# Strassen's quarter products for six of the sixteen feature tiles of a feed-forward layer's first part

## The chip, the core and the metric

The kernel runs on one core of a Trainium2 chip. A core has a matrix engine (PE, with its weight loads shown apart as PEld), three engines for element-wise work (DVE, ACT, POOL) and queues that issue transfers (here nearly all on SP). Every engine works through its instructions in the order in which the program issued them; what one engine needs of another it waits for. PE writes to PSUM, from where ACT or DVE copies results to SBUF. The metric is the time of one execution on the device in microseconds (us); lower is better.

## The reference

The input is q, k and v (8 batches, 8 heads, 576 positions, 64 features, float32) and a threshold `tau`. Attention with a threshold comes first, then a feed-forward layer on its output:

```python
scores = scale * np.matmul(q, k.transpose(0, 1, 3, 2))
thresh = np.max(scores, axis=-1, keepdims=True) - tau
scores = np.where(scores >= thresh, scores, -1000000000.0)
attn = np.exp(scores - np.max(scores, axis=-1, keepdims=True))
attn = attn / (np.sum(attn, axis=-1, keepdims=True) + 1e-09)
x = np.matmul(attn, v)                 # heads side by side: (8, 576, 512)

xn = (x - mean(x)) / np.sqrt(var(x) + 1e-06) * g_ln
out = x + np.maximum(xn @ w_ch1, 0.0) @ w_ch2      # 512 -> 2048 -> 512
```

## The kernel before, in words

**Slots and stages.** Attention is cut into 72 slots, nine to a batch (s = 0 to 8). In a slot, PE multiplies q and k for one piece of the batch's heads (scores, L390, 2.2 us); DVE takes the row maxima (L404) straight from PSUM; ACT takes exponentials (L415) with these as bias; DVE masks by the threshold and sums (L422); POOL scales by the reciprocal sums (L438); DVE transposes 32 x 32 blocks (`turn_blocks`, L498 and L504) into `et`; SP writes `et` to a scratch in memory and reads it back in another order in the next slot (`fetch`: `em`, and the last 64 positions into `rests`); in the last stage of that next slot PE multiplies with v (`values_of`, L550). Four slots of a batch also hold `turn` (L338 to L351), which prepares the next q and k. The first batch turns its weights with PE instead. Each slot is issued in four stages, 0 to 3: stage 0 ends between the second and the third exponential, stage 1 comes before the masks, stage 2 before the slot's transposes, stage 3 after them.

**Groups.** The feed-forward layer runs on 16 groups of 288 positions, two to a batch (even and odd), with features on the partitions. Its steps fill PE between the attention's products. `centre` subtracts the mean (`xc`, L599). `first_part` makes `hidden`, 16 tiles of 128 features: for each tile d, four products (one for each 128 input features, `product`, L101) into one PSUM bank, and an eviction by ACT with ReLU (L729). On the side it makes the variance: squares by ACT (L735), three sums by POOL (L737), a product with a constant (`var`), and an inverse square root by DVE in three rounds (`root`, L661 to L669).

The second part (`second_quarters`, all groups but the first) already uses Strassen's scheme: the 2 x 2 blocks of `w_ch2` (rows, columns) and of `hidden` (feature halves, early and late 144 positions) are combined so that seven block products, not eight, are needed. Sums of the weights are made once (`differences`, L706). Sums of `hidden` are made in place for each group: `t3` and `t4` on POOL, `t2` and `t1` on DVE (L797). Each of the seven products is a segment of 16 products of 144 columns. Then sums of their results (`u`, `22`, `21`, `11`, `12`, L816), scaling by the inverse root and adding x (`finish`: `done11`, `hi`, `done12` on POOL, L824 and L816), and output transposes on DVE (`store`: `o2`, `o3`, `o0`, `o1`, L643), after which SP sends them out (L650).

**The order.** PSUM has two banks for tiles, segments and the mean and variance products together (`ps_ff`, two buffers). A step to PE can therefore be started only when the step before the last has been evicted. The number of units issued in each stage follows a written rule (`second_part`, L900): what is left of the group, times the stage's share (0.6, 1.0, 1.25, 0.35), over the shares left until the next group is ready. A product of 288 columns is one unit, one of 144 columns half a unit; a group has 121 units.

Element-wise calls of a group wait in one queue, `drops`, in the order in which they were queued. `drip` (L608) takes them out at the end of stage 1 (only as far as an urgent call stands in the queue, and then with all that stand ahead of it), at the end of stage 2 (for up to 4 calls on DVE and 6 cost units on POOL) and of stage 3 (2 on DVE); before the masks only urgent calls for POOL go out. `need` takes out calls until a named one has gone. The order of a slot, shortened:

```python
diags = weights(es, thr, blocks_go)      # masks (DVE), scaling (POOL)
run_all(aside)
drip()                                   # end of stage 1
...
second_part(n, 2)
...
scr = turn_blocks(s, es)                 # the slot's transposes (DVE)
...
run_all(aside)                           # rounds of the root
drip({nc.vector: 4, nc.gpsimd: 6})       # end of stage 2
```

Of the kernel before, what the change touches and what calls it, by code (L numbers as in the profile page):

```python
# [18 lines left out]
def kernel(  # L19
# [39 lines left out]
    J = 4  # L59
# [7 lines left out]
    BIG = 3.0e38  # L67

# [19 lines left out]
    rests = [consts.tile([128, 4, 128], F32, name=f"rest{i}") for i in range(2)]  # L88
# [61 lines left out]
    for t in rests + v_rest:  # L150
        nc.gpsimd.memset(t, 0.0)
# [244 lines left out]
    def exponentials(n):  # L396
# [5 lines left out]
        for h in range(2):  # L402
            i = slice(2 * h, 2 * h + 2)
            nc.vector.tensor_reduce(  # L404
                out=neg[:, i], in_=pairs[h],
                axis=AXL.X, op=ALU.max, negate=True,
            )
            nc.gpsimd.tensor_scalar(  # L408
                out=thr[:, i], in0=neg[:, i], scalar1=-1.0, scalar2=low_sb,
                op0=ALU.mult, op1=ALU.add,  # L410
            )
        for i in range(4):
            if i == 2:
                yield es, thr
            nc.scalar.activation(es[:, i], blocks[i], func=AF.Exp, bias=neg[:, i : i + 1])  # L415

    def weights(es, thr, divide):
# [13 lines left out]
        for i in range(4):  # L431
            if not divide:
                if i % 2 == 0:
                    two = ffn.tile([128, TOK], F32, tag="o", bufs=4, name="diag")
# [14 lines left out]
    def turned_tiles(s):  # L449
        return att.tile([128, 4, J, 128], F32, tag="em", bufs=1, name="em"), rests[s % 2]  # L450
# [81 lines left out]
    def values_of(b, s, turned_weights):  # L532
# [23 lines left out]
        if s == HP:  # L556
            for t in range(2):
# [4 lines left out]
                for c in range(1, NK):  # L562
                    add_feature(2 * b + t, c, slice(QH, TOK))
        else:
# [3 lines left out]
            if hp:  # L568
                add_feature(g, hp, slice(0, QH))

    def add_feature(g, c, cols):

        x = groups[g]
        if g not in sums:
            sums[g] = ffn.tile([128, TOK], F32, tag="sum", bufs=2, name="sum")
# [59 lines left out]
    def add_to_x(g, m, p2, rb):  # L635
        o = ffn.tile([128, TOK], F32, tag="o", bufs=4, name="o")
# [4 lines left out]
    def store(eng, g, m, o):  # L641
        ot = ffn.tile([128, TOK], F32, tag="o", bufs=4, name="ot")
# [35 lines left out]
    HT, HD, HM = TOK // 2, ND // 2, NK // 2  # L678
# [5 lines left out]
    }  # L684
    more = []

    def differences():
# [5 lines left out]
        for t in (flat[:, :size], flat[:, size : 2 * size], flat4[:, :size]):  # L693
            more.append(t.rearrange("p (m d c) -> p m d c", m=HM, d=HD))
        s2, s3, s4 = more
# [13 lines left out]
    def first_part(g):  # L709
# [3 lines left out]
        rb = sq = None  # L713
        plain = g == 0
        sums_of = differences() if g == 1 else iter(())
        for d in range(ND):
            while conversion.ended < 4 * (d // 4 + 1):
                yield 0, 0
            while d == ND - 2 and len(rooted) <= g:
                run_all(aside)  # L720
# [9 lines left out]
            next(sums_of, None)  # L730
            yield 2, 1
            if sq is None and d and (plain or part > 1 or d == ND // 2 - 1):
                squared = d
                sq = hidden[:, ND - NK :]
                nc.scalar.activation(sq, xc, func=AF.Square)  # L735
                for c in range(1, NK):
                    nc.gpsimd.tensor_tensor(out=sq[:, 0], in0=sq[:, 0], in1=sq[:, c], op=ALU.add)  # L737
            elif sq is not None and rb is None and (
                d >= squared + (7 if plain else 3) and part > (0 if plain else 1)
                or d == ND - NK - 1  # L740
            ):
                var = ps_ff.tile([128, TOK], F32, tag="ff", name="var")
                product(var, lhsT=avg_sb, rhs=sq[:, 0], start=True, stop=True)
                rb = ffn.tile([128, TOK], F32, tag="rb", bufs=2, name="rb")
                nc.scalar.activation(sq[:, 2], var, func=AF.Identity, bias=eps_sb)
                aside.append(lambda: root(rb, sq[:, 2], sq[:, 3]))
                yield 1, 1
        for _ in sums_of:
            pass
        return rb  # L750

    def second_plain(g, rb):
        for m in range(NK):
# [10 lines left out]
            aside.append(lambda m=m, p2=p2: add_to_x(g, m, p2, rb))  # L764
            yield 2, 1

    def second_quarters(g, rb):
# [7 lines left out]
        drip(everything=True)  # L775
# [3 lines left out]
        done = set()  # L779

        def later(*calls, urgent=None):
            for what, cost, fn, eng, *args in calls:

                def go(what=what, fn=fn, eng=eng, args=args):
                    fn(eng, *args)
                    done.add(what)

                drops.append((urgent, now, eng, cost, go))

        def need(*what):  # L790
            while not done.issuperset(what):
                drops.pop(0)[-1]()

# [5 lines left out]
        def segment(weights, rhs, out=None):  # L799
# [10 lines left out]
            if out is None:  # L810
                out = ffn.tile([128, HM, HT], F32, tag="part", bufs=4, name="part")
            nc.scalar.copy(out, bank)  # L812
            return out

        def add(eng, out, a, b):
            eng.tensor_tensor(out=out, in0=a, in1=b, op=ALU.add)  # L816
# [11 lines left out]
        later(("t3", 3, by_fours, pool, b12, b22, b12, ALU.subtract), urgent=pool)  # L828
        banks_taken[0] = True
        yield from segment(w2[0, 0], b11, y11)  # L830
        need("t3")
        later(("t2", 3, by_fours, dve, b11, b11, b12, ALU.add), urgent=dve)
        yield 2, 0.5
        p2 = yield from segment(w2[0, 1], b21)
        need("t2")
        later(("t4", 3, by_fours, pool, b21, b21, b11, ALU.subtract), urgent=pool)
# [3 lines left out]
        yield from segment(s2, b11, y21)  # L840
        need("t4")
        later(("t1", 3, by_fours, dve, b11, b22, b11, ALU.subtract), urgent=dve)
# [218 lines left out]
```

## Time and profile before

| | |
|---|---|
| median of 3 runs | 1398.09 us (1396.95 to 1398.28) |
| profiled execution | 1397.5 us, span 1395.7 us |
| busy: PE, DVE, POOL, ACT | 1337.3, 931.2, 609.7, 460.4 us |
| products of 288 columns, tiles of the first part (`p<-xc,w`, 4 records each) | 4096 records, 518.1 us |
| products of 144 columns, segments (`seg<-hidden`, 4 records each) | 6720 records, 436.4 us |
| evictions with ReLU on ACT (L729) | 256, 414 ns each |
| copies of segments on ACT (L812) | 105, 400 ns each |
| sums of 288 columns, POOL (L816) and DVE (L668) | some 800 ns and 499 ns each |
| mean granted clock of PE | 0.993 |

The span is the time from the first to the last instruction; the profiled execution's own time is 1.8 us longer. One product shows as four records (two halves of the output columns, two records each), whose busy times overlap. In a line of the timeline the columns are start, duration, engine, line, operation, output and inputs, shape and count; in brackets stands how long the engine was idle just before and what ended it. After the first batch the kernel repeats: the row maxima of slots nine apart start 160.6 us apart.

### The profile page before, as it was taken

Reading aid. Unit: us, or ns where it says so; the run is one execution under the profiler, and the core shown is the slowest. Engines: PE = TensorE matmul, PEld = TensorE weight load, DVE = VectorE, ACT = ScalarE, POOL = GpSimd, SP = SyncE. Lnnn points to the kernel's source line nnn. Section 1 sums busy time; section 2 is a strip of 40 time slices with the busy share of each in tenths; the row PEclk is TensorE's granted clock in tenths of the full one; section 3 lists DMA queues with packets and bytes.
Section 4 is the critical chain, followed back from the end, with each engine's and each line's share of the span. In section 5 each row is a group of like instructions: output and inputs, shape, how many; then the busy total and the mean of one; then the engine's idle time right before and its main releaser. Section 6 shows DMA issues by size and latency. Waiting matters only on the chain.

```text
span 1395.7 us, 35606 instructions
## 1 busy us (share of the span) xinstructions
PE 1337.3 (96%) x15048; PEld 986.9 (71%) x15048; DVE 931.2 (67%) x1638; ACT 460.4 (33%) x923; POOL 609.7 (44%) x809
## 2 busy tenths in 40 slices
PE   4888999999999999999999999999999999999996
PEld 3665665867768596877869586776858677685966
DVE  5998967676776767657776767657775767766211
ACT  3877613232332323232232323323232323323120
POOL 2444444544433454343444455353444444334413
PEclk8999999999999999999999999999999999999998
DMA  9722355447744476446754477445764476443211
GB/s 231 175 77 70 95 145 153 154 146 187 196 133 159 136 191 180 142 137 185 192 160 146 150 196 188 138 148 151 187 180 143 134 183 184 127 161 129 63 18 18
DMA packets 316383, 205.48 MB, mean 147 GB/s; under 512 B 242368, under 2 KB 273856, under 8 KB 308160
## 3 DMA queue, kind: packets, MB, share of 16 engines
q1 hardware_dynamic: 311456, 202.62, 50.8%
q8 instruction: 118, 1.93, 0.6%
q10 hardware_dynamic: 4736, 0.59, 0.4%
q14 instruction: 41, 0.34, 0.1%
q0 software_dynamic: 32, 0.00, 0.0%
HBM read 119.41 MB, written 83.76 MB: 146 GB/s over the span
## 4 chain that ended last, share of the span: by engine, by line
PE 89%; DVE 5%; ACT 2%; issue 1%; POOL 0%; POOLq 0%; DVEq 0%; ACTq 0%
PE p L101 36%; PE seg L101 30%; PE sc L550 10%; PE sc L390 10%; DVE e L422 1%; PE tp L101 1%; DVE neg L404 1%; PE var L101 0%; PE mean L101 0%; DVE w L269 0%; ACT e L415 0%; PE tr L478 0%; ACT part L812 0%; DVE hidden L296 0%; DVE w L296 0%
## 5 line engine op out<-in xcount | busy, mean ns | idle before, releaser
L101 PE MATMUL p<-xc,w 128*64 128x288 f32 x4096 | 518.1, 408 | 13.0 <-ACT hidden L729 5.5
L101 PEld LDWEIGHTS p<-xc,w 128*64 128x64 f32 x4096 | 288.9, 137 | 224.6 <-ACT hidden L729 16.0
L404 DVE TENSOR_REDUCE neg<-sc 128x2 f32<-128x1152 f32 x144 | 188.8, 1352 | 271.1 <-PE sc L390 271.0
L415 ACT ACTIVATE e<-sc,neg 128x576 f32<-128x576 f32 x288 | 196.8, 744 | 247.7 <-DVE neg L404 247.7
L438 POOL TENSOR_SCALAR e<-e,den 128x576 f32<-128x576 f32 x252 | 194.1, 783 | 134.5 <-DVE den L427 134.3
L101 PE MATMUL seg<-hidden,w 128*64 128x144 f32 x3840 | 248.0, 287 | 0.0
L101 PEld LDWEIGHTS seg<-hidden,w 128*64 128x64 f32 x3840 | 235.1, 137 | 11.6 <-issue 7.7
L422 DVE SCALAR_TENSOR_TENSOR e<-sc,thr,e 128x576 f32<-128x576 f32 x288 | 222.0, 810 | 13.9 <-ACT e L415 13.2
L729 ACT ACTIVATE hidden<-p 128x288 f32<-128x288 f32 x256 | 105.9, 414 | 241.0 <-PE p L101 239.2
L408 POOL TENSOR_SCALAR thr<-neg,low_sb 128x2 f32<-128x2 f32 x144 | 42.5, 295 | 306.1 <-DVE neg L404 302.1
L390 PE MATMUL sc<-kT,qT 64*128 64x384 f32 (+3 forms) x1024 | 150.6, 425 | 20.1 <-DVE qT L350 10.1
L504 DVE STREAM_TRANSPOSE et<-e 128x1152 f32<-128x1152 f32 x112 | 153.1, 1374 | 14.8 <-POOL e L438 14.0
L390 PEld LDWEIGHTS sc<-kT,qT 64*128 64x128 f32 x1024 | 94.3, 191 | 69.9 <-issue 18.2
L550 PE MATMUL sc<-em,v_in 128*64 128x256 f32 (+1 forms) x1408 | 130.8, 329 | 0.0
L101 PE MATMUL seg<-hidden,stage 128*64 128x144 f32 x1920 | 123.1, 286 | 0.0
L101 PEld LDWEIGHTS seg<-hidden,stage 128*64 128x64 f32 x1920 | 117.9, 137 | 3.5 <-issue 2.3
L550 PEld LDWEIGHTS sc<-em,v_in 128*64 128x64 f32 x1408 | 86.4, 137 | 32.2
L797 POOL TENSOR_TENSOR hidden<-hidden 128x576 f32<-128x576 f32 x60 | 84.4, 1426 | 27.3 <-ACT hidden L729 19.0
L576 POOL TENSOR_TENSOR sum<-sum,x 128x256 f32<-128x256 f32 (+1 forms) x64 | 32.6, 509 | 113.2 <-ACT x L567 110.7
L797 DVE TENSOR_TENSOR hidden<-hidden 128x576 f32<-128x576 f32 x60 | 49.1, 853 | 47.8 <-PE seg L101 38.1
L567 ACT COPY x<-sc 128x256 f32<-128x256 f32 x60 | 22.3, 372 | 164.7 <-PE sc L550 115.3
L812 ACT COPY part<-seg 128x288 f32<-128x288 f32 x75 | 30.1, 401 | 131.2 <-PE seg L101 109.6
(151 smaller groups left out, 1186.6 us busy)
## 6 DMA issues: line engine op xcount, KB each, us to landing
scr<-et SPq DMA_DIRECT2D x63, 1152.0 KB, 4.9
em<-scr SPq DMA_DIRECT2D x63, 1024.0 KB, 5.9
out_dram<-ot SPq DMA_DIRECT2D x256, 36.0 KB, 4.9
q_in<-in_q_dram SPq DMA_DIRECT2D x124, 72.0 KB, 2.7
k_in<-in_k_dram SPq DMA_DIRECT2D x120, 72.0 KB, 3.0
rest<-scr SPq DMA_DIRECT2D x63, 128.0 KB, 6.0
v_in<-in_v_dram SPq DMA_DIRECT2D x28, 256.0 KB, 5.2
w<-in_moe_w_ch_dram SPq DMA_DIRECT2D x10, 512.0 KB, 6.2
```

The lines of the kernel that those rows point to most:

```text
L101: nc.tensor.matmul(out[r], lhsT=lhsT[:, r], rhs=rhs, **flags)
L390: nc.tensor.matmul(sc[h][64 * i : 64 * i + 64 if s == HP else 128, at : at + n], lhsT=ql[r] if s == HP else qT[r, half, j * 128 : (j + 1) ...
L404: nc.vector.tensor_reduce(out=neg[:, i], in_=pairs[h], axis=AXL.X, op=ALU.max, negate=True,)
L408: nc.gpsimd.tensor_scalar(out=thr[:, i], in0=neg[:, i], scalar1=-1.0, scalar2=low_sb, op0=ALU.mult, op1=ALU.add,)
L415: nc.scalar.activation(es[:, i], blocks[i], func=AF.Exp, bias=neg[:, i : i + 1])
L422: nc.vector.scalar_tensor_tensor(out=es[:, i], in0=blocks[i], scalar=thr[:, i : i + 1], in1=es[:, i], op0=ALU.is_ge, op1=ALU.mult, accum_o ...
L438: nc.gpsimd.tensor_scalar(out=es[:, i], in0=es[:, i], scalar1=den[:, i : i + 1], scalar2=1.0, op0=ALU.mult, op1=ALU.mult,)
L504: nc.vector.transpose(et[:, :, 64 * h : 64 * h + 64].rearrange("p n (j c) -> p j n c", j=2), es[:, 2 * h : 2 * h + 2].rearrange("p j (n c) ...
L550: nc.tensor.matmul(dst[64 * h : 64 * h + 64], lhsT=vt[:, h, c, :] if c < J else vr[:, h, :], rhs=pick(em[:, :, c] if c < J else er, hp, h) ...
L576: nc.gpsimd.tensor_tensor(out=sums[g][:, cols], in0=x[:, 0, cols] if c == 1 else sums[g][:, cols], in1=x[:, c, cols], op=ALU.add,)
L729: nc.scalar.activation(hidden[:, d], p1, func=AF.Relu)
L797: eng.tensor_tensor(out=out[at], in0=in0[at], in1=in1[at], op=op)
```

## The change

Tiles 5, 6, 7 and 13, 14, 15 of the first part are made by Strassen's scheme, like the second part. The 2 x 2 blocks are of `w_ch1` (256 input features by 384 features) and of `xc` (256 input features by 144 positions). Seven quarter products `Q1` to `Q7` of six products of 144 columns each take the place of 24 products of 288 columns. Group 0 keeps whole tiles.

- Weight sums are made once, in group 1, into tiles of their own (`w1_more`); one of them is in place. `differences` is stepped three times a tile instead of once.
- Sums of `xc` go into parts of `hidden` not yet in use: `xt3`, `xt2`, `xt4` (POOL, queued as urgent when the quarters start) and `xt1` (DVE).
- Results are copied by ACT without ReLU and combined by `xu2`, `xu3`, `x21`, `x12`, `xu4`, `x22` (DVE) and `x11` (POOL); `r11` (POOL), `r21`, `r12`, `r22` (DVE) clamp them at zero.
- The ten whole tiles run first; from the third on, one quarter product follows each.
- A group has 118 units.
- The variance may start one stage earlier (`part` instead of `part > 1`), and its product one tile earlier.
- The second part no longer empties the queue at its start; some of its results go straight into `y`.
- To make room: one tile for the remainders instead of two (`er`), one `sum` buffer instead of two, two `part` buffers of 432 columns instead of four of 288, and no `o` buffers: the output transposes write into the group's x tile. Sums for the last 32 positions of an odd group move from s = 4 to s = 6. From the second batch on there is a second place in each slot where finished outputs are sent.

```diff
-    rests = [consts.tile([128, 4, 128], F32, name=f"rest{i}") for i in range(2)]
+    er_sb = consts.tile([128, 4, 128], F32, name="er")
...
+        if s == HP + 2:
+            add_rest(g)
...
-            sums[g] = ffn.tile([128, TOK], F32, tag="sum", bufs=2, name="sum")
+            sums[g] = ffn.tile([128, TOK], F32, tag="sum", bufs=1, name="sum")
...
-        ot = ffn.tile([128, TOK], F32, tag="o", bufs=4, name="ot")
+        ot = groups[g][:, m]
...
+            for k in range(NK // 2):
+                s1 = of(1, 0, k)
+                nc.gpsimd.tensor_tensor(out=s3[k], in0=of(0, 0, k), in1=s1, op=ALU.subtract)
+                yield
+                nc.vector.tensor_tensor(out=s1, in0=s1, in1=of(1, 1, k), op=ALU.add)
+                nc.vector.tensor_tensor(out=s2[k], in0=s1, in1=of(0, 0, k), op=ALU.subtract)
+                nc.gpsimd.tensor_tensor(out=s4[k], in0=of(0, 1, k), in1=s2[k], op=ALU.subtract)
+                yield
...
+        def norm(must=False):
+
+            if ended and not squared and (plain or part):
+                squared.append(ended)
+                nc.scalar.activation(sq, xc, func=AF.Square)
+                for c in range(1, NK):
+                    nc.gpsimd.tensor_tensor(out=sq[:, 0], in0=sq[:, 0], in1=sq[:, c], op=ALU.add)
+            elif squared and not rb and (
+                ended >= squared[0] + (7 if plain else 2) and part > (0 if plain else 1) or must
+            ):
+                var = ps_ff.tile([128, TOK], F32, tag="ff", name="var")
+                product(var, lhsT=avg_sb, rhs=sq[:, 0], start=True, stop=True)
...
+        def quarter(q, weights, rhs, out=None):
+            bank = ps_ff.tile([128, size, HT], F32, tag="ff", name="quarter")
+            for k in range(half):
+                for m in range(size):
+                    at, end = (k, m), (half - 1, size - 1)
+                    product(
+                        bank[:, m], lhsT=weights[k][:, m * 128 : (m + 1) * 128], rhs=rhs[:, k],
+                        start=at == (0, 0), stop=at == end,
+                    )
+                    if at != end:
+                        yield 1, 0.5
+            if out is None:
+                out = part_tile("part")[:, : size * HT].rearrange("p (m t) -> p m t", t=HT)
+                parts[q] = out
+            nc.scalar.copy(out, bank)
+            yield 2, 0.5
+
+        def quarters():
+            later(
+                done, ("xt3", 1, less, pool, t3, b22, b12), ("xt2", 1, add, pool, t2, b11, t3),
+                ("xt4", 1, less, pool, t4, b21, t2), urgent=pool,
+            )
+            yield quarter(1, old(0, 0), b11, h11)
+            yield quarter(2, old(0, 1), b21)
+            need(done, "xt4")
+            yield quarter(7, s3, t3)
+            later(done, ("xt1", 1, less, dve, t1, b12, b11), urgent=dve)
+            yield quarter(6, s2, t2, h12)
+            later(
+                done, ("xu2", 1, add, dve, h12, h12, h11), ("xu3", 1, add, dve, parts[7], parts[7], h12),
+                ("x11", 1, add, pool, h11, h11, parts[2]), ("r11", 1, positive, pool, h11),
+            )
+            need(done, "xt1")
+            yield quarter(4, old(1, 1), t4, h21)
+            later(done, ("x21", 1, add, dve, h21, h21, parts[7]), ("r21", 1, positive, dve, h21))
+            need(done, "x11")
+            yield quarter(3, s4, b22)
+            later(done, ("x12", 1, add, dve, h12, h12, parts[3]))
+            yield quarter(5, old(1, 0), t1, h22)
+            later(
+                done, ("xu4", 1, add, dve, h12, h12, h22), ("r12", 1, positive, dve, h12),
+                ("x22", 1, add, dve, h22, h22, parts[7]), ("r22", 1, positive, dve, h22),
+                urgent=dve,
+            )
...
+        for d in singles:
...
+            yield from tile_of(d)
+            for _ in range(1 if plain else 3):
+                next(sums_of, None)
+            ended += 1
+            yield from norm()
+            if not plain and d > 1:
+                yield from next(between, ())
+                yield from norm()
...
-        drip(everything=True)
...
-    STEPS = [1 + NK * ND * 2] + [1 + NK * ND * 2 - NK * ND // 8] * (NG - 1)
+    STEPS = [1 + NK * ND * 2] + [
+        1 + NK * ND * 2 - NK * ND // 8 - sum(NK * len(ms) for ms in SETS) // 4
+    ] * (NG - 1)
...
+        if n >= SLOTS:
+            run_first(stores)
```

## The prediction

> **What bounds the kernel now.** I read the head of the page, then the time by stretches, the chain that ended last, and the timeline of single slots. The head:
>
> ```profile
> span 1395.7 us, 35606 instructions
> PE 1337.3 (96%) x15048; PEld 986.9 (71%) x15048; DVE 931.2 (67%) x1638; ACT 460.4 (33%) x923; POOL 609.7 (44%) x809
> ```
>
> PE is busy 96% of the span. One batch of nine slots, as a stretch (columns: stretch, length, busy time and instructions of PE, PEld, DVE, ACT, POOL, clock, DMA):
>
> ```profile
> 530.60:691.20 160.60, 159.97 (x1826) 118.49 (x1824) 109.37 (x196) 47.51 (x96) 72.47 (x100) 1.00 0.56 163
> ```
>
> So a batch is as long as PE's work in it. DVE has 51 us to spare, but on average only. The chain in order of time shows PE alone, with these prices:
>
> ```profile
> 1171.79 11.79 PE p L101 x96
> ...
> 1355.84 27.46 PE seg L101 x448
> ```
>
> 96 matmul records are 24 products of 288 columns: 11.79 / 24 = 0.491 us. 448 are 112 products of 144 columns: 27.46 / 112 = 0.245 us.
>
> DVE in a slot of s = 2, where an odd group begins (its scores ended at 368.75):
>
> ```profile
> 368.92 2.62 DVE L404 TENSOR_REDUCE neg<-sc 128x2 f32<-128x1152 f32 x2 [2.93 <-PE sc L390]
> ...
> 376.83 1.38 DVE L504 STREAM_TRANSPOSE et<-e 128x1152 f32<-128x1152 f32 x1
> 378.49 1.38 DVE L504 STREAM_TRANSPOSE et<-e 128x1152 f32<-128x1152 f32 x1 [0.28 <-POOL e L438]
> 379.79 1.96 DVE L816 TENSOR_TENSOR y<-y,part 128x288 f32<-128x288 f32 x3
> 384.53 0.84 DVE L643 STREAM_TRANSPOSE ot<-y 128x288 f32<-128x288 f32 x2 [2.78 <-POOL y L816]
> 386.16 0.48 DVE L643 STREAM_TRANSPOSE ot<-y 128x288 f32<-128x288 f32 x1 [0.79 <-POOL y L816]
> 386.95 2.62 DVE L404 TENSOR_REDUCE neg<-sc 128x2 f32<-128x1152 f32 x2 [0.31 <-PE sc L390]
> ```
>
> Here DVE has 0.31 us left before the next row maxima, though it stood still 2.78 and 0.79 us in front of the output transposes, which wait for POOL. ACT in the next slot:
>
> ```profile
> 388.41 1.37 ACT L415 ACTIVATE e<-sc,neg 128x576 f32<-128x576 f32 x2 [3.24 <-DVE neg L404]
> 389.67 0.41 ACT L729 ACTIVATE hidden<-p 128x288 f32<-128x288 f32 x1
> ```
>
> The eviction that frees PE's PSUM bank stands behind two exponentials, and these behind the maxima. There are two banks, so maxima that come late stop PE.
>
> **The gain.** Fifteen groups each lose 24 products (24 x 0.491 = 11.8 us) and get 42 half-width ones (42 x 0.245 to 0.248 = 10.3 to 10.4): 1.4 us each, 21 us in all, all of it on PE's path.
>
> **What else is added.** ACT: six evictions of 0.41 become seven of 432 columns, 0.50 by interpolation between 288 (0.40) and 512 (0.59): 1.0 us a group on an engine busy 47.5 of 160.6. DVE a group: one sum of 288 (0.45), six of 432 (0.58, between 0.45 and 0.70), three clampings (0.4 by L661's 0.37): 5.1 us. POOL: three of 288 (0.80), one of 432 (1.1), one clamping (0.6): 4.1 us. By throughput this fits; its place decides.
>
> **Without cost.** One remainder tile instead of two: its fetch stands on SP behind that of `em`, which has one tile and waits for the same slot's reads. One `sum` tile: the mean's product has read it before the next group's first sum. The output transposes write the group's own x tile, which the third group after needs: the last send goes in the slot s = 4 (odd) or s = 8 (even), the tile is written again at the earliest in stage 3 of the slot after an even group's or two slots after an odd one's; SP has the same 256 sends, two send points a slot. `part` with two buffers: each is read out a segment before it is due. The exponentials keep their order.
>
> **Where it lands: odd groups.** The pacing rule (L900) issues a group's units by fixed shares. In the slot s = 2 it gives 8, 5, 11, 4 units in stages 0 to 3; the trace's 24 products in a row there are 8 + 5 + 11. With 118 units instead of 121 it gives 8, 5, 10, 4. Three tiles are 12 units, so the quarter generator starts on the 13th, in stage 1, and queues `xt3`, `xt2`, `xt4` as urgent. The drip at the end of stage 1 then pushes out all ahead of them: `22`, `21`, `hi`, `12`, `done12` and four output transposes. That is ahead of the slot's own transposes (L504), which came first before. Also `part` instead of `part > 1` puts the square and its three POOL sums ahead of POOL's scaling of e, and the square root falls one slot earlier.
>
> From the start of the maxima: ACT's exponentials end at 5.7, the square at 6.8 (1.16), POOL's three sums at 9.5 (2.65), the scalings at 12.4 (2.95), `hi` at 15.4 (1.56 + 1.40), `done12` at 17.1. DVE ends the masks at 7.9, three sums at 9.9, waits for `hi`, two transposes to 16.3, waits for `done12`, two more to 18.0; the slot's transposes to 20.8 (2.76), the root's first two rounds to 24.1 (3.3), the third to 25.5 (1.4). The next maxima are due at 18.0: 7.5 us late. Queued behind DVE's wait are thus the transposes, the root and the next maxima; behind the maxima ACT's exponentials and the evictions of `Q7` and `p8`. PE's cover is these two steps, 7 units or 3.45 us, against 0.17 + 2.8 + 0.5 us until the first eviction even when punctual. PE stands 7.5 us; a wait of 0.5 us which that slot has now goes. 7.0 us x 6 groups (3, 5, ... 13) = 42 us. The variance product waits for the square's sums (9.5 against 9.05): 0.45 x 6 = 2.7.
>
> A stand this long has a row (columns: stretch, length, PE busy, clock, DMA); PE stood from 14.3 to 21.5 us:
>
> ```profile
> 16.00:20.00 4.00, 0.00 (x0) 0.79 1.12 348
> 20.00:24.00 4.00, 2.48 (x7) 0.50 1.15 278
> 24.00:28.00 4.00, 4.00 (x21) 0.50 0.97 156
> 28.00:32.00 4.00, 3.57 (x60) 0.93 1.08 344
> ```
>
> After it the granted clock was 0.50 for 7.0 us more (21.5 to 28.5): 3.5 us lost. At 3.5 us x 6 that is 21 us, bounded by 0 and by 45 if the stands of 3 us below do it too. [...]
>
> **Where it lands: odd groups, second place.** In the slot s = 4 (six times) `r11` is dripped after stage 1, so on POOL behind the scaling, which ends 8.0 us after the scores; `r11` ends at 8.75. PE comes to the first segment's tile 5 after `Q5` (1.5), `p12` (2.0), the bank's wait and ten half products (2.5): 6.0. 2.75 x 6 = 16.5 us; 0 if `r11` came before the scaling, 3.8 a slot if POOL's scaling is as slow as where L438 takes 2.48 us for two (1.47 otherwise).
>
> **Even groups.** In s = 6, stage 3, the drip likewise takes `12`, `done12` and the transposes together, behind the root, which has moved there: variance evicted at 17.0 us after the maxima began, root to 20.3, `12` to 20.8, `done12` on POOL to 22.4, transposes to 23.3, where the maxima now start at 20.1 (7.55 us idle before them). 3.1 us late, PE's cover is again used up, 0.5 us of wait goes: 2.6 x 7 = 18 us.
>
> **Group 1** has the one-time weight differences, three a tile instead of one, with eight new ones of 384 columns: POOL falls behind its slot by some 3 us. I take 3, between 0 and 6.
>
> **Sum** against the profiled execution (1397.5 us, span 1395.7): 1397.5 - 21 + 42 + 2.7 + 21 + 16.5 + 18 + 3 = 1479.7. The median of the runs shown is 1398.09, 0.6 us higher: 1480.
>
> **Rivals.** (1) Milder: `xt3` is queued a unit later, in stage 2, and the push comes behind the slot's transposes. Then 10.9 + 3.3 + 1.9, wait, transposes to 18.0, third round to 19.4: 1.9 us late, no clock drop. 1397.5 - 21 + 6 x 1.9 + 16.5 + 18 + 3 = 1425. For it: the margin is one unit. Against: the rule is arithmetic, and its counts fit the rows. (2) Faster: the queue's push costs PE nothing, because DVE's lateness stays within the cover. This decides from a lateness under about 0.5 us, that is, if `hi` and `done12` ran before the scaling or the transposes were not in the queue. Then 1398 - 21 = 1377. For it: 51 us of free DVE time a batch; against it the 0.31 us in the row above. (3) Worse: the clock also falls after the 3 us stands, 13 x 1.9 us by the same half rate, and POOL and DVE slow each other: 1505 to 1520. (4) No change: gain and waits cancel, only with about a quarter of the waits.
>
> **How the numbers follow.** As worked out, 1445 to 1515: 0.67. Milder, 1400 to 1445: 0.17, some three quarters of it above 1415. Faster: 0.10. Above 1515: 0.04. Within 0.2% (2.8 us, about what a measurement of this kernel can tell from no change): 0.02. The range 1415 to 1515 holds 0.8. Slower by over 0.2%: 0.88.
>
> **What would show it.** In the profile after: PE's busy share falls below 92%; the list of waits has PE behind ACT's evictions for 50 us or more, in stands of 7 us once and 3 us once a batch; the granted clock drops in one place a batch; DVE's output transposes wait for POOL and stand ahead of the slot's transposes; the first segment waits for POOL's clamping. Products of 144 columns that cost more than 0.25 us, or no idle PE at s = 3, would make the prediction wrong.

## The result, and the profile after

The changed kernel takes 1529.95 us (median of 4 runs, 1528.87 to 1531.13) against 1398.07 us (4 runs, 1396.95 to 1398.28): a ratio of 1.0945, 95% interval 1.0926 to 1.0964. The prediction was slower, 1480 us, at most 1515. The direction and the places were right; the time lies 15 us outside the range.

The head of the page after:

```profile
span 1529.2 us, 38142 instructions
...
PE 1366.7 (89%) x16128; PEld 1068.6 (70%) x16128; DVE 1050.8 (69%) x1792; ACT 478.5 (31%) x938; POOL 704.9 (46%) x887
```

PE's busy share fell from 96 to 89%. Of the 133.5 us that the span gained, 104.1 are idle time of PE (162.5 against 58.4) and 29.4 are busy time: the products became cheaper, but a part of them ran at a granted clock of 0.50. Where PE waits, from the list of waits (us in total, times, longest):

```profile
PE quarter L104 <- ACT part L831: 43.4, 12, 7.1
PE p L104 <- ACT hidden L800: 31.4, 9, 3.9
PE seg L104 <- POOL hidden L761: 26.4, 6, 4.4
```

One batch of nine slots, as a stretch with the columns of the prediction; before it was 160.60 long with PE busy for 159.97 at clock 1.00:

```profile
595.30:776.11 180.81, 164.26 (x1968) 129.81 (x1969) 125.50 (x216) 49.69 (x99) 84.68 (x110) 0.95 0.50 144
```

The batch has three stands. From the timeline of PE in the same batch (start, length, what runs, and in brackets how long PE stood before it and for whom):

```profile
595.30 3.15 PE L104 MATMUL quarter<-hidden,w 128*64 128x144 f32 x24 [7.14 <-ACT part L831]
...
622.11 5.81 PE L104 MATMUL seg<-hidden,w 128*64 128x144 f32 x64 [4.40 <-POOL hidden L761]
...
678.93 4.11 PE L104 MATMUL p<-xc,w 128*64 128x288 f32 x16 [3.70 <-ACT hidden L800]
```

They open the slots s = 3 and s = 7 and the second part at s = 4, the places that the prediction named. VectorE in the slot s = 2 ahead of the first one (its maxima began at 566.44):

```profile
574.31 2.24 DVE L755 TENSOR_TENSOR y<-y,part 128x288 f32<-128x288 f32 x3
582.13 0.84 DVE L651 STREAM_TRANSPOSE x<-y 128x288 f32<-128x288 f32 x2 [5.58 <-POOL y L755]
583.76 0.84 DVE L651 STREAM_TRANSPOSE x<-y 128x288 f32<-128x288 f32 x2 [0.79 <-POOL y L755]
584.52 2.59 DVE L507 STREAM_TRANSPOSE et<-e 128x1152 f32<-128x1152 f32 x2
...
591.65 2.62 DVE L407 TENSOR_REDUCE neg<-sc 128x2 f32<-128x1152 f32 x2
```

Counted from 566.44, the output transposes begin at 15.7, the slot's own end at 20.7, and the next maxima begin at 25.2, where the prediction worked out 15.4, 20.8 and 25.5. Before, the output transposes came last and waited 2.78 us for GpSimd, with 0.31 us to spare before the next maxima.

The clock, from half-microsecond stretches of PE around the 4.40 us stand, which PE ended at 622.11 (stretch, length, PE busy, granted clock, DMA):

```profile
622.00:622.50 0.50, 0.39 (x6) 1.00 0.00 0
622.50:623.00 0.50, 0.50 (x10) 0.67 0.00 0
...
624.00:624.50 0.50, 0.50 (x8) 0.50 0.00 0
...
626.00:626.50 0.50, 0.50 (x10) 0.92 0.00 0
```

The clock fell here at 622.67, when PE had been at work again for 0.6 us, and came back 3.4 us later. Behind the first 30 us, all 22 stands of 2.7 us or more but one, not the 7 us ones alone, were followed by such a drop, of 1.4 to 2.8 us of lost time. Summed over PE's busy time at the lower clock, the loss is 45 us in this execution and 3.5 us in the profiled one of before.

### The profile page after: what moved, and what is told of

Read it like the earlier page. It is cut to its first block, busy times and chain, and to the rows that moved or that the text cites. A ratio compares the mean times of both kernels' runs of the same rounds, so it can differ in the third digit from the quotient of the medians.

```text
span 1529.2 us, 38142 instructions
## 1 busy us (share of the span) xinstructions
PE 1366.7 (89%) x16128; PEld 1068.6 (70%) x16128; DVE 1050.8 (69%) x1792; ACT 478.5 (31%) x938; POOL 704.9 (46%) x887
## 3 DMA queue, kind: packets, MB, share of 16 engines
q8 instruction: 127, 2.08, 0.6%
## 4 chain that ended last, share of the span: by engine, by line
PE 63%; DVE 16%; POOL 9%; ACT 5%; issue 3%; DMA 2%; SPq 1%; POOLq 0%; DVEq 0%; ACTq 0%
PE seg L104 24%; PE p L104 16%; PE sc L553 8%; PE sc L393 7%; PE quarter L104 6%; DVE neg L407 3%; ACT e L417 3%; DVE e L425 2%; POOL e L441 2%; DVE hidden L673 2%; DMA em<-scr 2%; DVE et L507 1%; POOL y L940 1%; POOL y L755 1%; DVE hidden L676 1%
## 5 line engine op out<-in xcount | busy, mean ns | idle before, releaser
L104 PE MATMUL p<-xc,w 128*64 128x288 f32 x2656 | 366.5, 424 | 38.5 <-ACT hidden L800 31.4
L104 PEld LDWEIGHTS p<-xc,w 128*64 128x64 f32 x2656 | 194.9, 143 | 164.8 <-ACT hidden L800 36.6
L104 PE MATMUL seg<-hidden,w 128*64 128x144 f32 x3840 | 259.4, 294 | 28.3 <-POOL hidden L761 26.4
L104 PEld LDWEIGHTS seg<-hidden,w 128*64 128x64 f32 x3840 | 245.3, 141 | 40.7 <-POOL hidden L761 28.0
L441 POOL TENSOR_SCALAR e<-e,den 128x576 f32<-128x576 f32 x252 | 199.2, 801 | 124.6 <-DVE den L430 124.4
L393 PE MATMUL sc<-kT,qT 64*128 64x192 f32 (+3 forms) x1024 | 149.0, 424 | 19.6 <-DVE qT L353 10.0
L104 PE MATMUL quarter<-hidden,w 128*64 128x144 f32 x1440 | 113.7, 311 | 44.8 <-ACT part L831 43.4
L104 PEld LDWEIGHTS quarter<-hidden,w 128*64 128x64 f32 x1440 | 100.0, 150 | 66.4 <-POOL thr L411 44.3
L800 ACT ACTIVATE hidden<-p 128x288 f32<-128x288 f32 x166 | 68.8, 415 | 160.0 <-PE p L104 159.2
```

Of the source, the lines that this page charges most:

```text
L104: nc.tensor.matmul(out[r], lhsT=lhsT[:, r], rhs=rhs, **flags)
L393: nc.tensor.matmul(sc[h][64 * i : 64 * i + 64 if s == HP else 128, at : at + n], lhsT=ql[r] if s == HP else qT[r, half, j * 128 : (j + 1) ...
L441: nc.gpsimd.tensor_scalar(out=es[:, i], in0=es[:, i], scalar1=den[:, i : i + 1], scalar2=1.0, op0=ALU.mult, op1=ALU.mult,)
L800: nc.scalar.activation(hidden[:, d], p1, func=AF.Relu)
```

## The experiments

Theory: the order of issue makes the waits. The urgent sums push the closing work ahead of VectorE's slot work, the norm moved a stage earlier, r11 stands behind the scaling; each stand then costs a clock drop too. Rival: VectorE and GpSimd are too full, with 125.5 and 84.7 us of work a batch instead of 109.4 and 72.5, whatever the order. On the clock: a drop after long stands alone, or a loss that grows with the stand. Line numbers in a run's rows are its own. A time without a range is that of one execution; where a kernel was run several times, its times lay within 0.6% of each other.

**r11 ahead of the scaling.**

```diff
-            need(done, "x11")
+            need(done, "r11")
             yield quarter(3, s4, b22)
```

> The change with POOL's clamping r11 put ahead of the slot's scaling (it is issued together with x11). Theory, that the order of issue makes the waits: the stand of 4.40 us in front of the first segment's products (six times 4.40 = 26.4 us) goes, and with it a clock loss of 1.7 us each, 10 us in all, so some 36 us off 1530: 1494 us, while the stands at the head of s = 3 (7 us) and s = 7 (3.6 us) stay as they are. Rival, that VectorE and GpSimd are simply too full: the clamping takes the same time on GpSimd wherever it stands, its 2.1 us come back as lateness of something else, and the time stays above 1520.

1493.28 us. The wait for GpSimd's clamping is gone from the list; the other two stand as before:

```profile
PE quarter L104 <- ACT part L831: 43.4, 12, 7.1
PE p L104 <- ACT hidden L800: 31.4, 9, 3.9
```

Six stands of 4.40 us and their clock were worth 36.7 us. In the change the clamping took 2.08 to 2.09 us in its six rows at s = 4, where sums and a clamping of VectorE ran beside it throughout, and 1.65 to 1.67 in its nine others.

**The norm as late as before.**

```diff
-            if ended and not squared and (plain or part):
+            if ended and not squared and (plain or part > 1 or ended >= 5):
...
-                ended >= squared[0] + (7 if plain else 2) and part > (0 if plain else 1) or must
+                ended >= squared[0] + (7 if plain else 3) and part > (0 if plain else 1) or must
```

> The change with the square, its three sums and the variance product issued as late as in the kernel before (part > 1, three tiles between), nothing else moved. Theory of order: without 2.65 us of sums ahead of the scaling and without the root's 3.3 us in the slot, the maxima of s = 3 come at most 0.5 us late instead of 7.2, and those of s = 7 at most 0.8 us late instead of 4.3. The stands of 7.0 x 6 and 3.6 x 7 go, with clock losses of 1.7 x 6 and 2.6 x 7: 42 + 25 + 10 + 18 = 95 us, so about 1435 us (1425 to 1455). The stand of 4.40 us at s = 4 stays. Rival of fullness: the same work is done in the next slot and makes that one late; less than half of it comes back, above 1480 us.

1451.31 us, 79 us back where 95 were expected. The waits of PE that are left:

```profile
PE seg L104 <- POOL hidden L761: 26.5, 6, 4.4
PE p L104 <- ACT hidden L800: 15.0, 8, 3.9
...
PE quarter L104 <- ACT part L831: 6.7, 13, 0.7
```

At s = 3 0.7 us stays, at s = 7 1.39 us six times: the push is still there, and costs this much without the norm ahead of it. None of the 1.39 us stands was followed by a clock drop. VectorE in the slot s = 2 (its maxima began at 548.17):

```profile
561.19 0.84 DVE L651 STREAM_TRANSPOSE x<-y 128x288 f32<-128x288 f32 x2 [3.51 <-POOL y L755]
...
566.11 2.58 DVE L407 TENSOR_REDUCE neg<-sc 128x2 f32<-128x1152 f32 x2
```

The output transposes still wait 3.51 us for `hi`, and yet the next maxima begin after 17.9 us, as they are due. The change had 7.3 us more there: 4.6 are the root's rounds ahead of the maxima (587.04 to 591.65), 2.1 the longer wait for `hi`, behind the norm's sums, and 0.6 the closing sums, which took 2.24 instead of 1.64 us.

**The urgent sums at the head of the list**, the norm still early.

```diff
+        new = []
...
-            drops.append((urgent, now, eng, cost, go))
+            new.append((urgent, now, eng, cost, go))
+        if ahead:
+            drops[:0] = new
+        else:
+            drops.extend(new)
...
-                ("xt4", 1, less, pool, t4, b21, t2), urgent=pool,
+                ("xt4", 1, less, pool, t4, b21, t2), urgent=pool, ahead=True,
```

> The change with one edit: xt3, xt2 and xt4 go to the head of the list, so that the push takes nothing else with it; the norm stays early and r11 behind the scaling. It fills the last field of four: at the head of s = 3 PE stood 7.0 us with the push and the early norm, 0.7 us at most with the push and the late norm, 2.66 us without the push and with the late norm. Worked out from the start of the maxima as in the prediction, with the durations of the change's own trace: scalings to 12.4, the three xt sums to 15.0, hi to 17.8, done12 to 19.5 on GpSimd; on VectorE the transposes to 13.9, the root to 17.2, the three closing sums to 19.5, the last root round and three output transposes to 22.4, where the next maxima are due at 18.0: 4.4 us late, a stand of some 4.2 us. At s = 7 the output transposes have left the slot and 0 to 1 us stays. The stand of 4.40 at s = 4 stays. So 1530 - 6 x 2.8 - 7 x 3 - 7 x 2.6 = 1474 us (1455 to 1485): the early norm makes the larger part of the wait, the push alone next to none. If the push were the cause, the stand at s = 3 would be gone, below 1445 us.

1507.54 us: a miss of 33 us. The stand moved to a place that I hadn't thought of. ACT and then PE, at the head of s = 3:

```profile
579.86 0.52 ACT L836 COPY part<-quarter 128x432 f32<-128x432 f32 x1 [7.63 <-DVE y L760]
```

```profile
580.70 2.21 PE L393 MATMUL sc<-kT,qT 64*128 64x384 f32 x16 [3.54 <-ACT x L570]
```

The second quarter's copy needs the buffer `part` that the closing sums of the group before still read, and these had gone behind the transposes and the root on VectorE. ACT stood 7.63 us for it, the values' copy behind it on ACT, and the scores of s = 3 behind that. The prediction had put the two `part` buffers down as free of cost; that holds for the order of the change alone.

**Three edits of order together**: the three diffs above in one kernel.

> The change with three edits of order alone: the norm as late as before, the sums xt3, xt2, xt4 put at the head of the list (so that the push takes nothing else with it), and r11 ahead of the scaling. Every instruction of the change is still there. Theory of order: all three kinds of stand go; what stays are group 1 (10.6 us of stands and some 5 us of clock) and the gain of the products (between 10 and 21 us), and perhaps 1 us a batch at s = 8, where the four output transposes now stand: 1398 - 10 to 21 + 15 + 0 to 7 = 1392 to 1410 us, VectorE's busy time unchanged at 1050 us. Rival of fullness (16 us more of VectorE a batch is what costs): above 1480 us.

1420.84 us (1419.06 to 1422.46), ratio to before 1.0171 (1.0154 to 1.0188). Every instruction of the change is in it, VectorE is busy for 1044.8 us, and 109 of the 132 us are gone: the rival of fullness falls. What kept it from 1410 is one stand of 2.66 us at s = 3, six times, four of them with a clock drop. VectorE stood 4.41 us there for `hi`, and GpSimd shows why:

```profile
551.35 0.80 POOL L763 TENSOR_TENSOR hidden<-xc 128x288 f32<-128x288 f32 x1
...
553.98 2.85 POOL L784 TENSOR_TENSOR hidden<-hidden 128x288 f32<-128x288 f32 x3
556.79 1.40 POOL L945 TENSOR_TENSOR y<-y,rb 128x576 f32<-128x576 f32 x1
```

The three xt sums and the norm's sums stand ahead of `hi`. So the four runs give the stand at the head of s = 3:

| | norm early | norm late |
|---|---|---|
| push takes the closing work along | 6.87 to 7.14 (the change) | 0.7 |
| sums alone go first | 3.54, ahead of the scores, then 0.7 or less (four times) or 3.4 (twice) | 2.66 |

With the push, the early norm makes the difference between 0.7 and 7 us. What the early norm costs without the push the table doesn't show: the only order that was tried without it brings waits of its own, 2.66 us with the norm late.

**The order without the work.** The kernel before, with no Strassen product in its first part:

```diff
-        drip()
+        drip(everything=s == 2 and n > 2 * SLOTS)
...
+            early_norm = g > 2 and g % 2
-            if sq is None and d and (plain or part > 1 or d == ND // 2 - 1):
-                squared = d
+            if sq is None and d and (plain or part > (0 if early_norm else 1) or d == ND // 2 - 1):
+                squared = d - (1 if early_norm else 0)
```

> The kernel before, without a single Strassen product or sum of the first part, with the order of the change alone in the slot s = 2 of six batches: the list is emptied at the end of stage 1 (the closing sums, hi, done12 and the four output transposes ahead of the slot's own transposes), and the square, its sums and the variance product are issued one stage earlier. Theory of order: the stand of 7 us at the head of s = 3 appears in it, six times, with a clock loss of 1.7 us each: 1398 + 6 x (7.0 - 0.5) + 6 x 1.7 = 1447 us. Rival of fullness: there is no added work, so nothing changes, 1396 to 1405 us.

1444.81 us, 47.7 above its own runs of before (1397.12). VectorE waits the same 5.58 us for `hi` as in the change:

```profile
544.54 2.23 DVE L817 TENSOR_TENSOR y<-y,part 128x288 f32<-128x288 f32 x3
552.35 0.84 DVE L643 STREAM_TRANSPOSE ot<-y 128x288 f32<-128x288 f32 x2 [5.58 <-POOL y L817]
```

PE stood 4.06 us at s = 3 and 1.67 us in front of the variance product, six times each, with 1.4 to 2.9 us of clock behind the former and none behind the latter. The total met the forecast of 1447, but not by a single stand of 7 us: this order gives 5.7 us in two places where the change has 6.9 to 7.1 in one.

**The work without its sums.** The sums and clampings that combine the seven quarters are left out, so six feature tiles are not computed; the sums ahead of the products and the rest of the order stay.

```diff
-            later(
-                done, ("xu2", 1, add, dve, h12, h12, h11), ("xu3", 1, add, dve, parts[7], parts[7], h12),
-                ("x11", 1, add, pool, h11, h11, parts[2]), ("r11", 1, positive, pool, h11),
-            )
...
-            later(done, ("x21", 1, add, dve, h21, h21, parts[7]), ("r21", 1, positive, dve, h21))
-            need(done, "x11")
...
-            later(done, ("x12", 1, add, dve, h12, h12, parts[3]))
...
-            later(
-                done, ("xu4", 1, add, dve, h12, h12, h22), ("r12", 1, positive, dve, h12),
-                ("x22", 1, add, dve, h22, h22, parts[7]), ("r22", 1, positive, dve, h22),
-                urgent=dve,
-            )
```

> The change without the sums and clampings that put the seven quarter products together (xu2, xu3, x11, r11, x21, r21, x12, xu4, r12, x22, r22): six feature tiles are left wrong in it. The sums ahead of the products, all products and the order of everything else stay. VectorE loses 4.6 us of work a group, GpSimd 2.8. Theory of order: the stands at the head of s = 3 (7 us) and s = 7 (3.6 us) are there as before, only the one at s = 4, which waits for r11, goes: 1490 to 1497 us, as with r11 put first. Rival of fullness: with most of the added VectorE work gone, the stands at s = 3 and s = 7 shrink by as much or go, below 1450 us.

1480.43 us. VectorE is busy for 954 us instead of 1051, nearly as little as before, and the stands at s = 3 (6.9 us six times) and s = 7 (3.65 us) are all there:

```profile
PE quarter L104 <- ACT part L831: 41.2, 6, 6.9
PE p L104 <- ACT hidden L800: 33.1, 9, 5.6
```

Of the 13 us to r11 put first, 11 are clock: 24 us lost at the lower clock against 35, with stands of the same length at s = 3 and s = 7.

**The price of a stand.** The kernel before, with spare work on VectorE ahead of the maxima of s = 3:

```diff
+        for _ in range((0, 0, 14, 4, 24, 7, 18, 10)[b] if s == 3 else 0):
+            nc.vector.transpose(spare, w1_sb[0][:, :192])
         scores(b, s)
```

> The kernel before, with a number of VectorE transposes of 128 x 192 into a spare tile put ahead of the maxima of the slot s = 3, a different number in each batch: 14, 4, 24, 7, 18, 10 in batches 2 to 7, some 0.31 us each, worked out between the row of 288 columns (0.42) and that of 1152 (1.38). That makes VectorE late by 4.4, 1.3, 7.5, 2.2, 5.6 and 3.1 us less the 0.3 us that it has free. Theory: PE's cover is used up there, so each stand is the lateness plus the half microsecond that PE waits there anyway, 4.6, 1.5, 7.7, 2.4, 5.8 and 3.3 us, 22 us in all; and the clock drops after every stand of 2.8 us or more, for 1.3 to 2.9 us of loss, whatever its length: 8 to 12 us, so 1397 + 22 + 9 = 1428 us. Rival one, that a longer stand loses more clock: the loss grows from about 1 us at 3 us to 3.5 us at 7.7 us. [...] Rival three, that PE has cover: the first doses cost nothing.

1428.12 us. One transpose took 0.41 us, not 0.31. Two of the rows:

```profile
714.98 9.84 DVE L959 STREAM_TRANSPOSE spare<-w 128x192 f32<-128x192 f32 x24
724.74 2.58 DVE L405 TENSOR_REDUCE neg<-sc 128x2 f32<-128x1152 f32 x2
```

| transposes | 4 | 7 | 10 | 14 | 18 | 24 |
|---|---|---|---|---|---|---|
| PE stood, us | 0.32 | 1.56 | 2.81 | 4.44 | 6.09 | 8.57 |
| clock lost after it, us | 0 | 0 | 0 | 2.60 | 1.80 | 1.74 |

Each further transpose adds its 0.41 us to the stand, but for about 1 us that PE has to spare in this kernel: beyond that, lateness of the maxima is paid in full. The loss of clock doesn't grow with the stand, so rival one on the clock falls, and of rival three only that 1 us is left. A drop after long stands alone fits this run, with drops after 4.44 us and more and none after 2.81, but not the drops after 2.66 us in the run with three orders. The total met the forecast through two errors of opposite sign, the transpose too cheap and the clock loss (6.1 us against 8 to 12) too dear.

**The order repaired.** The xt sums go directly ahead of the output transposes in the list (so `hi` and `done12` come first on GpSimd and the output transposes stay behind the slot's own), norm late, r11 first, and the one-time differences are spread:

```diff
+        at = len(drops)
+        if ahead:
+            at = next((i for i, d in enumerate(drops) if d[-1].what[0] == "o"), at)
...
-            drops.append((urgent, now, eng, cost, go))
+            go.what = what
+            drops.insert(at, (urgent, now, eng, cost, go))
+            at += 1
```

> The change with four edits of order and place: the norm late and r11 ahead of the scaling as in the run with three orders; the sums xt3, xt2, xt4 put directly ahead of the four output transposes in the list, so that the push takes the closing sums, hi and done12 with it but leaves the transposes behind the slot's own; and the one-time weight differences spread, those of the first layer over group 0's second part, those of the second layer one behind each tile and quarter of group 1. No instruction is dropped. Theory of order: the stand of 2.66 us at the head of s = 3 that was left with three orders (GpSimd's hi stood behind the norm's sums and the xt sums) goes with its clock losses, 16 + 7 us, and most of group 1's (5.6 + 3.1 us and 3 us of clock): 1421 - 23 - 9 = 1389 us, between 1380 and 1398, so that the gain of the products, 16 us, is what is left of the change. Rival of fullness: VectorE's and GpSimd's added work shows somewhere else, 1410 us or more.

1399.74 us (11 runs, 1398.20 to 1402.34), ratio 1.0016 (1.0007 to 1.0025), where 1380 to 1398 was expected. In the steady part the change is now worth 1.43 us a batch. One batch:

```profile
698.73:857.89 159.16, 157.78 (x1971) 125.69 (x1969) 123.66 (x215) 49.88 (x98) 84.94 (x110) 1.00 0.56 165
```

159.16 us against 160.59 in the same slots of before, no stand over 0.6 us, clock 1.00, with VectorE as full as in the change. All the rest, 14 us, is lost by n = 13: 10.4 of them in the slots n = 10 to 13, where group 1's weight differences on GpSimd make VectorE wait, 3 in clock drops ahead of n = 7, after stands that the kernel before has too.

**Group 1, twice.** The first attempt moved the differences to slots with idle time on the average, one engine's waiting for the other's.

```diff
+                four_of(w2_sums[0])
+                ahead.append(next(between))
...
+            if m == 2:
+                run_out(differences_1())
```

> The kernel of the run that spread the differences out, with group 1 given room: the first layer's differences all behind the third tile of group 0's second part, where VectorE has 3.2 and GpSimd 2.0 of 10 us of work in the run with three orders; group 1's xt sums in the slot before, where GpSimd stands still for 4.4 us; four of the second layer's sixteen differences there too, the other twelve at the end of the first part and behind the first two segments. In the run before, the slots n = 10 to 13 took 10.4 us more than in the kernel before (1.0, 2.6, 6.8), while each later batch took 159.16 us against 160.60. Theory: the 10 us are lateness of VectorE behind GpSimd's differences, so 6 to 11 of them go, and the whole change is then worth its products: 1400 - 9 = 1391 us (1386 to 1396), 0.1 to 0.8% below the kernel before. Rival: VectorE has no room in these slots either way, the lateness moves on to n = 13 and 14, 1398 us or more.

1404.29 us, ratio 1.0051 (1.0037 to 1.0064): wrong. VectorE stood 8.1 and 8.5 us for differences of GpSimd that came behind other work, and in n = 13 the differences stood ahead of t3, for stands of 2.8 and 3.4 us and 3.4 us of clock (not the 8 us that the next forecast names). The second put each ahead of what its engine had to wait for anyway:

```diff
+                if (m, d) == (2, 3):
+                    differences_1()
...
+        if g == 1:
+            w2_sums.append(differences())
+            some_of(w2_sums[0], 8)
```

> As in the run that gave group 1 room, but with the differences where their engine stands still and nothing waits behind them: the first layer's in the third quarter of the slot n = 9, all subtractions of GpSimd ahead of what VectorE needs of them (in the run before VectorE waited 8.1 us for GpSimd there, and 2.9 us of PE's time went with it), the second layer's first eight ahead of group 1's square in n = 10 (VectorE waited 8.5 us for GpSimd there), the next four at the end of the first part, the last four behind the third and fourth segment (before, they stood ahead of t3, and PE lost 2.8 + 3.4 us of stands and 8 us of clock in n = 13 and 14). Theory: what is left of group 1 are waits of 1 to 3 us, and the 1.44 us a batch of the products show: 1404 - 14 = 1390 us (1385 to 1395). Rival, no room: 1398 us or more.

1395.68 us (12 runs, 1391.95 to 1399.85), ratio to before 0.9986 (0.9977 to 0.9995): the change in this order is faster than the kernel before by 0.14%, less than the 1390 us expected. Up to n = 15 it still loses 7 us to before.

## Why the prediction was right and wrong

- **Where it lands** was right in all three places, and for the stated reason. At s = 3 the chain on VectorE came within 0.3 us of its working (25.2 against 25.5), six stands of 6.86 to 7.14 us, 41.5 us in all where 42 were expected. That these agree is in part luck: the sum took 0.5 us off each stand of 7.5 for a wait that was to go, and the profile of before has no such wait at s = 3; its one wait of 0.57 us a batch, in s = 6, is still there in the change. The kernel before with the order alone has VectorE's wait of 5.58 us and 5.7 us of stands, so this chain needs none of the added products, and the run without the combining sums that it needs none of those.
- **The clock** is the step that failed most. I took 3.5 us after the 7 us stands alone, 21 us in all, and put the loss after the 3 us stands, 1.9 us each by an estimate of mine, into a rival with a small chance. It was 45 us, some 42 more than before: 1.4 to 2.8 us after the stands of 7, of 4.4 and of 3.6 us alike. That is 21 us of the 50 by which the sum was short. The one row that I had, a 7.25 us stand at the start, gave the loss of a single stand too high and said nothing of short ones. My upper bound of 45 us for this term was about right; the range did not take it in.
- **r11** was mis-sized. I took 0.6 us for the clamping, and the sum left 0.75 for it (8.0 to 8.75); it took 2.09 us there (1.66 undisturbed), behind a scaling of 1.79 instead of 1.47 us:

```profile
616.53 1.47 POOL L441 TENSOR_SCALAR e<-e,den 128x576 f32<-128x576 f32 x2 [1.74 <-DVE den L430]
618.21 1.79 POOL L441 TENSOR_SCALAR e<-e,den 128x576 f32<-128x576 f32 x2 [0.21 <-DVE den L430]
619.97 2.09 POOL L761 TENSOR_SCALAR hidden<-hidden 128x432 f32<-128x432 f32 x1
```

  4.40 us six times, 26.4 against 16.5 us; the missing 1.65 us are 1.34 of the clamping and 0.3 of the scaling. The row that I had scaled from multiplies by a scalar in each partition; the clamping is another operation with two constants.
- **Even groups**: maxima 4.3 us late instead of 3.1, because the root took 4.4 us instead of 3.3. Six stands of 3.62 to 3.70 us and one of 2.77, 24.7 us, where 18 were expected; here too the 0.5 us that the sum took off each stand was not there to go.
- **Group 1** cost 10.6 us up to n = 15 instead of 3 (0 to 6), about half of it in stands (3.13 and 3.92 us, where before had 1.77) and 4.4 in the clock drops behind them: VectorE waited 5.2 us for GpSimd's scaling of q_in behind the differences, which the sum had left out.
- **The gain** was 16 us, not 21. PE's busy time in a batch at full clock fell by 2.19 us (159.97 to 157.78 in the repaired order), 1.10 a group. Six products of a quarter took 1.47 to 1.57 us there from their start to that of the next (0.251 each on the average, about at the 0.25 us that the prediction had named as a sign against it), not 0.245 to 0.248; these came from runs of 112 in a row, and quarters stand alone between tiles. Of the 1.10 us, 0.4 go into small waits even there, so 0.72 a group arrive.
- **The variance product** cost 1.2 us instead of 2.7.

The terms together, against the 133.5 us of the span: idle time of PE 41.5 (s = 3) + 26.4 (r11) + 24.7 (even groups) + 1.2 (variance) + 5.3 (group 1's stands) = 99.1 of 104.1, the rest in waits of 0.1 to 0.6 us and one of 1.6; busy time 42 of clock less 16 of gain, 26 of 29.4.

## What to carry to other kernels

Where several engines work in order, cost an added operation by what is queued behind it and by what it waits for, not by the engine's free time: the same instructions gave 1530 and 1396 us in two orders. A flush of "urgent" work takes along all that stands ahead of it, and the same flush cost 0.7 us with the norm late and 7 us with the norm early. Count the clock with each stand of PE: here each of 33 stands of 4.05 us or more was followed by a drop, in the change for 1.7 to 2.7 us of lost time, and 3 of 6 stands of 2.44 to 2.54 us were. And keep one-time work out of the slots where two engines pass results to each other.

## What the runs showed of the hardware

- **Whether a stand was followed by a clock drop went by where it fell, not by its length alone.** Behind the first 30 us, stands of 4.05 us or more were followed by a drop in all 33 cases (12 in the change, 6 each with the norm late, with the order without the work and with the sums at the head of the list, 3 with the spare transposes), of 3.62 to 3.70 in 5 of 6 (the change), of 2.66 in 4 of 6 (three orders), of 2.44 to 2.54 in 3 of 6 (sums at the head of the list), of 2.81 in none (one case, the spare transposes), of 1.67 or less in none of the steady part. In the change the loss was 1.71 to 1.82 us behind 13 of 22 drops and 1.41 to 2.75 behind the others, and the drops behind stands of 2.7 us or more began 2.0 to 5.1 us after PE had stopped, often with PE at work again. The clock's records show an order in this: within one execution the drops begin at whole multiples of 3.41 us from each other and last 3.41, 6.83 or 10.24 us (44 drops behind the first 30 us: 22 in the change, 19 with the sums at the head of the list, 3 with the spare transposes; in the batch above at 591.95, 622.67 and 677.28 us, 9 and 16 times 3.413 apart). In these three traces and that of before, a stretch of 3.41 us between two such points that began at full clock and in which PE stood for 2.05 us or more was always followed by a drop, one with less than 1.82 us never. So a stand that was cut in two by such a point, the one of 3.63 us without a drop in the change (1.78 and 1.85 us), went free. Of the stand of 7.25 us at the start, the traces of before and of the spare transposes show a drop; in the change the clock's records begin only after it, at 25.3 us, so they show nothing on it.
- **A drop ahead of another wait took the place of that wait.** With the sums at the head of the list, the second stand at s = 3 was 0.34 to 0.71 us in the four batches where the clock had dropped before it, for a loss of 2.7 to 3.1 us, and 3.35 and 3.37 us in the two where it had not: 3.4 us either way. Behind these two then came a drop of their own, of 2.9 and 3.0 us.
- **Beside each other, instructions of GpSimd and VectorE took longer.** In the change, VectorE's sums of 128x432 took 0.57 to 0.61 us with nothing of GpSimd beside them, and 0.98 to 1.07 where GpSimd's scaling ran beside them throughout. Two of those scalings took 1.79 us there at s = 4 instead of 1.47, and up to 2.10 with the sums at the head of the list. Why was not tried.
- **A clamping on GpSimd** took 1.66 us for 432 columns (median of 15 in the change), where VectorE took 0.46 for as many (median of 45) and GpSimd's scaling 0.74 for 576. What makes it so was not tried.
